# T5 attention and a bilinear feed-forward layer on one core: one weighted-value matmul for both heads' tail queries, and two groups of transposes at other places

## The chip, the core and the metric

The kernel runs on one core of a Trainium2 chip. A core has a matrix engine (TensorE, PE in the profile; its weight loads are listed apart as PEld), three engines for elementwise work (VectorE = DVE, ScalarE = ACT, GpSimd = POOL) and SyncE (SP). Each engine works through its own list of instructions in order and waits on semaphores for the others. Transfers are issued by SP, ACT and POOL and carried by 16 DMA engines. SBUF is the on-chip memory of 128 partitions; PSUM is the memory into which TensorE writes.

The metric is the device time of one execution in microseconds (us). Before the change it is 418.68, the median of four runs.

## What is computed

Attention over 8 batches and 8 heads, 576 positions and head size 64, with a relative-position bias that depends on the distance alone, and then a feed-forward layer without a nonlinearity but the product of its two halves:

```
scores = q @ k.T / sqrt(64) + bias_table[bucket(|i - j|)]   # per batch and head
attn   = exp(scores) / sum(exp(scores))                     # max subtraction cancels
x      = (attn @ v) with heads side by side                 # 4608 x 512
out    = ((x @ w_a) * (x @ w_b)) @ w_out                    # 512 -> 1536 -> 512
```

Beyond a distance of about 128 all positions share the last bucket. The kernel divides the bias of that bucket out, so that only a band around the diagonal has to be multiplied by exp(bias); the whole of it is read from tables `W_sb` and `Wt_sb`.

## The kernel before

**Tiles.** 576 positions are four tiles of 128 (NM = 4) and a tail of 64 (ST). Two heads make a pair, so there are 32 pairs; `p` is a pair, `b, hp = divmod(p, 4)` its batch and its place in it. Scores are computed transposed: keys on the partitions, queries along the columns. For a pair, `qk` (L407) makes for each key tile `t` a PSUM tile `sc` with both heads' 512 main queries, and `ex` (L429, ACT) makes `at` from it with one exponential of 1024 columns; `mul` (L434, DVE) multiplies by the bias table.

**The tail.** The tails of both heads lie together in 128 partitions: head 0 in rows 0 to 63, head 1 in rows 64 to 127. In `ZB` tail queries and tail keys stand block-diagonally. `qk_tail` (L478 to L493) makes the scores of the tail keys, `ex_tail` (L508, L515, L516) their exponentials, into the row buffer `att`. Tail queries against main keys come from `qk` (L416) and `ex_rows` (L423) in later batches, from L485 in the first two. In `att` the columns of these rows are ordered head, key tile, query: 256 columns of head 0 and then 256 of head 1. `mul_tail` (L524) multiplies the band of the tail keys by 192 columns of `Wt_sb`.

**Weighted values.** `av_mm` makes up to three query tiles (`jq`) in one PSUM tile `av`, of which there is one. Each `jq` starts with the tail keys against both heads' tail values (L561, 130 columns: 2 x 65, the 65th being a column of ones that gives the sum), and then adds, per head and key tile, a matmul of 65 columns (L565). That holds for jq = 4, the tail queries, too: there the eight matmuls take from `att` 128 columns at `256 * hh + 64 * t`, of which the first 64 belong to the tile, and only rows 0 to 63 of the result are used. `av_norm` takes the reciprocal of the sums (L579) and multiplies (L580) into `XG[p % 2]`, for jq = 4 by a reciprocal and a product of their own on 64 partitions.

**Transposing x.** `t_x` brings the result, transposed, into `xn_sb`, the operand of the feed-forward layer. For pairs 4 to 30, except 7, SP does it by two DMA transposes (L588, L591). For pairs 0 to 3, 7 and 31 TensorE does it (`tr_x`, L606) through a half of the PSUM tile `trb`, and `copy_x` (L299 on DVE) copies it out. `t_pair` calls it, for pair 7 in two parts one right after the other: tiles 0 to 2, then tiles 3 and 4.

**Transposing q and k.** For batches 0 and 1 TensorE does it. From batch 2 on POOL loads half a batch at a time (`load_half`: k in four pieces, q in four, the tails, v), and `t_half(b, g)` lets SP issue two DMA transposes (L379: `KB` from `kn`, then `QB` from `qn`), for the first half also the tails' (`t_tails`, L371: `ZB` from `tl`). SP's transfers are issued in the order of the program, and a waiting one holds those behind it.

**Order.** The program order is written by hand. The opening, which covers the scores of pairs 0 to 7 and the values of pairs 0 to 5, is a string of tokens: `S`, `T` scores, `E`, `ET` exponentials, `M`, `MT` products, `AV` weighted values, `N` normalisation, `FA`, `FB`, `HA`, `G` feed-forward. Behind `N41` and `N51` come pair 4's and pair 5's `t_x`. After the string `t_half(2, 0)` is called. Then a loop runs over slots `s` = 7 to 32. A slot makes the rest of pair `s`'s scores (`qk(s, ...)`, `qk_tail`) and the weighted values of pair `s - 1`; between them stand places `U` for the feed-forward layer. The layer's work is cut into units: `pa` or `pb` (L630, four matmuls of 512 columns, followed by a copy `ha` on ACT or a product `g` on DVE), and `po` (L667), three units to a tile, the third followed by a copy `ob` (L672) and an output transfer (L675) on ACT. A slot's nine units are dealt evenly over its places:

```
n = (quota * seen + nu - 1) // nu - put
```

**Buffers.** Two PSUM tiles `sc` for scores: a score group can start when the exponential of the last but one has read its tile. One tile `av`: the next weighted-value group waits for the normalisation of the last one.

Of the kernel before, what the change touches and what calls it, by code (L numbers as in the profile page):

```python
# [13 lines left out]
def kernel(  # L14
# [66 lines left out]
    eb_sb = const.tile([128, H], BF16, name="eb_sb")  # L81
    tab_sb = const.tile([128, TB], BF16, name="tab_sb")
    zero_sb = const.tile([128, 512], BF16, name="zero_sb")
    tab = nc.dram_tensor("bias_tab", [H, TB], BF16, kind="Internal")
    NY = S + NM
    W_sb = [wpool.tile([128, 2, NY], BF16, name=f"W{hp}") for hp in range(H // 2)]
    Wt_sb = wpool.tile([128, H // 2, 192], BF16, name="Wt")

# [22 lines left out]
    wb_sb = [wpool.tile([128, NMC, WC], BF16, name=f"wb{i}") for i in range(NW)]  # L111
    wo_sb = wpool.tile([128, NDF, DM], BF16, name="wo")
    xn_sb = [wpool.tile([128, NT], BF16, name=f"xn{mc}") for mc in range(NMC)]
    ob_last = wpool.tile([128, DM], FP32, name="ob_last")
# [87 lines left out]
    def pad_x(i):  # L202
        nc.vector.memset(XG[i][64:128, 4, :, :], 0.0)
        nc.vector.memset(att[i][:, 512 + SM // 2 + ST:], 0.0)

# [39 lines left out]
    def load_wt(hh):  # L245
        nc.gpsimd.dma_start(out=Wt_sb[64 * hh:64 * hh + 64, :, :],
                            in_=bass.AP(tensor=tab, offset=hh * TB + 512,
                                        ap=[[1, 64], [2 * TB, H // 2], [1, 192]]))
# [171 lines left out]
    def ex_rows(p):  # L420
        st[p]["att"] = at = att[p % 2]
        for hh in (1, 0):
            nc.scalar.activation(out=at[:, 256 * hh:256 * hh + 256], in_=st[p]["rows"][hh][:, 0:256],  # L423
                                 func=ACTF.Exp, scale=scale)

# [48 lines left out]
    def qk_tail(p):  # L474
        qT, kT, z = operands(p)
        ps = ps_sc.tile([128, 2, 512], FP32, tag="sc", name=f"qkt{p}")
        if shared(p):
            nc.tensor.matmul(out=ps[:, 0, :], lhsT=z[:, 1, :], rhs=qT[:, :, :], start=True, stop=True)  # L478
            for hh in range(2):
                nc.tensor.matmul(out=ps[:, 1, 0:ST], lhsT=z[:, 1, :], rhs=z[:, 0, ST * hh:ST * hh + ST],  # L480
                                 start=(hh == 0), stop=(hh == 1))
            st[p]["ps"] = (ps, None)
            return
        for t in range(NM):
            nc.tensor.matmul(  # L485
                out=ps[:, 0, :].rearrange("p (h t c) -> p h t c", h=2, t=NM)[:, :, t, :],
                lhsT=kT[:, t, :], rhs=z[:, 0, :], start=True, stop=True)
        n = main_tail(p)
        nc.tensor.matmul(out=ps[:, 1, 0:n], lhsT=z[:, 1, :], rhs=qT[:, (SM - n) // 128:, :],
                         start=True, stop=True)  # L490
        pt = ps[:, 1, n:n + ST] if n < SM else tr_half().bitcast(FP32)[:, 0:ST]
        for hh in range(2):
            nc.tensor.matmul(out=pt, lhsT=z[:, 1, :], rhs=z[:, 0, ST * hh:ST * hh + ST],  # L493
                             start=(hh == 0), stop=(hh == 1))
        st[p]["ps"] = (ps, pt)
# [5 lines left out]
    def ex_tail(p):  # L501
        ps, pt = st[p]["ps"]
        n = main_tail(p)
        at = att[p % 2]
        m = 512 + n
        st[p]["att"] = at
        if shared(p):
            nc.scalar.activation(out=at[:, 512:m + ST],  # L508
                                 in_=ps[:, :, :].rearrange("p a x -> p (a x)")[:, 0:SM + ST],
                                 func=ACTF.Exp, scale=scale)  # L510
            return
        if n < SM:
            m += ST
        else:
            nc.scalar.activation(out=at[:, m:m + ST], in_=pt, func=ACTF.Exp, scale=scale)  # L515
        nc.scalar.activation(out=at[:, 0:m], in_=ps[:, :, :].rearrange("p a x -> p (a x)")[:, 0:m],  # L516
                             func=ACTF.Exp, scale=scale)

    def mul_tail(p):
        if not shared(p):  # L520
            mul_rows(p)
        at, wt = st[p]["att"], Wt_sb[:, p % 4, :]
        o = 512 + main_tail(p) - 128
        nc.vector.tensor_tensor(out=at[:, o:o + 192], in0=at[:, o:o + 192], in1=wt[:, 191::-1], op=MULT)  # L524

    def mul_rows(p):
        at, w = st[p]["att"], W_sb[p % 4]
        x = at[:, 0:512].rearrange("p (h t c) -> p h t c", h=2, t=NM)
        rev = w[:, :, ST - 1::-1]
        e = bass.AP(tensor=rev.tensor, offset=rev.offset,  # L530
                    ap=[rev.ap[0], rev.ap[1], [1, NM], rev.ap[2]])
        nc.vector.tensor_tensor(out=x, in0=x, in1=e, op=MULT)

    def weights(p, t, hh, jq):
        if jq == 4:
            o = 256 * hh + ST * t
            return st[p]["att"][:, o:o + 128]
        if p >= 4:
            return st[p]["at"][t][:, hh, 128 * jq:128 * jq + 128]
        o = 256 * (t % 2) + 128 * (jq % 2)  # L540
        return st[p]["at", jq // 2, t // 2][:, hh, o:o + 128]

    def weights_tail(p, jq):
        if jq == 4:
            o = 512 + main_tail(p)
            return st[p]["att"][:, o:o + 128]
        if p < 4 and jq < 2:
            return atk[:, p, 128 * jq:128 * jq + 128]
        o = 512 + 128 * (jq if p >= 4 else jq - 2)
        return st[p]["att"][:, o:o + 128]  # L550
# [5 lines left out]
    def av_mm(p, jqs, pool=None, tag="av"):  # L556
        b, hp = divmod(p, 4)
        i = b % 2
        pav = (pool or ps_av).tile([128, 3, 2, Dh + 1], FP32, tag=tag, name=f"av{p}_{jqs[0]}")
        for slot, jq in enumerate(jqs):  # L560
            nc.tensor.matmul(out=pav[:, slot, :, :], lhsT=weights_tail(p, jq),  # L561
                             rhs=vt[i][:, hp, :, :], start=True, stop=True)
            for hh in range(2):
                for t in range(NM):
                    nc.tensor.matmul(out=pav[:, slot, hh, :], lhsT=weights(p, t, hh, jq),  # L565
                                     rhs=vm[i][:, 2 * hp + hh, t, :], start=False,
                                     stop=True, skip_group_check=True)
        st[p]["pav", jqs[0]] = pav

    def av_norm(p, jqs):  # L570
        pav = st[p]["pav", jqs[0]]
        rc = wrk.tile([128, 3, 2], FP32, tag="rc", name=f"rc{p}_{jqs[0]}")
        xg = XG[p % 2]
        groups = [(jqs[0], 0, len(jqs), 128)]
        if jqs[-1] == 4:
            groups = [(jqs[0], 0, len(jqs) - 1, 128), (4, len(jqs) - 1, 1, 64)]
        for j0, s0, n, np_ in groups:
            r = rc[0:np_, s0:s0 + n, :]
            nc.vector.reciprocal(out=r, in_=pav[0:np_, s0:s0 + n, :, Dh])  # L579
            nc.vector.tensor_tensor(  # L580
                out=xg[0:np_, j0:j0 + n, :, :], in0=pav[0:np_, s0:s0 + n, :, 0:Dh],
                in1=r.unsqueeze(3).to_broadcast([np_, n, 2, Dh]), op=MULT)

    def t_x(p, jqs=range(5), eng=None):
# [11 lines left out]
        copy_x(p, jqs, eng)  # L596

    def t_pair(p):
        for jqs in ((0, 1, 2), (3, 4)) if p == 7 else (range(5),):
            t_x(p, jqs)  # L600

# [113 lines left out]
    def v_next(s):  # L715
# [15 lines left out]
        N00 TZ0 E301 M100 X00 S201 CX00:D AV10 wa4 E201 M200 N10 CZ0:A M201 X10 TQ11 M301 CX10:A T0 CQ11:A  # L731
        V1:D TQ31 ET0 S111 M010 AV20 E111 MT0 T1 N20 AV30 CQ31:A ET1 M011 TQ21 LH S110 N30 X20 CQ21:A
        S310 CX20:A MT1 X30 E110 AV01 CX30:D M111 FA0a E310 M110 S210 FB0a N01 HA0a S211 E210 FA1a G0a
# [5 lines left out]
        CQ6:A FB2b MT4 E51 TQ7 G2b AV40 CQ7:D E50 TK6 M51 TK7 CK6:A FA3b M50 FB3b HA3b CK7:D S61 G3b T5  # L739
        E61 N40 FA4b FB4b HA4b M61 T6 ET5 G4b AV41 FA5b ET6 N41 S63 FB5b MT5 HA5b S62 E63 FA6b G5b MT6  # L740
        AV50 HA6b M63 E62 S60 FB6b N50 E60 FA7b G6b AV51 M62 HA7b FB7b M60 FA8f G7b N51 FB8f HA8f G8f
# [5 lines left out]
    def step(token):  # L747
# [79 lines left out]
        elif kind == "PC":  # L827
            if p == 2:
                pad_ones(1)
            else:  # L830
                nc.vector.memset(vt[1][64 * p:64 * p + 64, :, 1 - p, :], 0.0)
        elif kind == "PD":
            pad_x(p)
        elif kind == "LH":
            load_half(2, 0)
            load_half(2, 1)
        elif kind == "LV":
            load_vt(2)
        else:
            raise ValueError(token)  # L840
# [3 lines left out]
    pad_tl(1)  # L844
    t_half(2, 0)

    quotas = {7: 9, 8: 9}
    load_slot = {bb: 9 if bb == 3 else 12 if bb == 4 else 4 * bb - 5 for bb in range(3, B)}
    for s in range(7, NP + 1):
# [6 lines left out]
        if new:  # L856
            head = [U, lambda: ex(s, 1), A(0, 1, 2), U, lambda: mul(s, 0), lambda: t_q(s + 1), U,
                    lambda: mul(s, 1)]
            late = [A(3, 4), lambda: t_pair(s - 1), U]
            if shared(s):  # L860
# [67 lines left out]
```

## Time and profile before

| | us |
|---|---|
| median of 4 runs | 418.68 (418.57 to 419.3) |
| the profiled execution's own time | 418.99 |
| its span in the trace | 417.2 |
| DVE, ACT, POOL busy | 237.5, 250.0, 134.1 |

Times below are counted from the span's start. The span is what the program's instructions cover; the profiled execution took 1.8 us more than it. The "busy" share is an average over the whole program; what an engine waits for stands in brackets behind a row of the timeline: idle time before it, and the event that ended it. The granted TensorE clock was 0.998 of the full one.

```profile
L565 PE MATMUL av<-vm,at 128*128 128x65 bf16 x896 | 41.2, 194 | 0.0
L561 PE MATMUL av<-vt,att 128*128 128x130 bf16 x152 | 33.3, 219 | 0.0
L606 PE MATMUL trb<-ident,XG 128*128 128x128 bf16 x30 | 3.6, 219 | 2.0 <-DVE xn L299 1.1 <-ACT xn L297 0.4 <-DVE XG L580 0.3
L480 PE MATMUL qkt<-ZB 128*128 128x64 bf16 x48 | 5.3, 193 | 0.0
```

These are rows of the table of groups by line and shape: line, engine, operation, output and inputs, shapes and count, then the group's busy time in us and the mean length of one in ns, then idle time before it and what ended it. The length of a matmul runs from its start to its modelled end, with its way through the array, so neighbours overlap; what a matmul takes from the engine is the distance between starts.

### The profile page before, as it was taken

Reading aid. Unit: us, or ns where it says so; the run is one execution under the profiler, and the core shown is the slowest. Engines: PE = TensorE matmul, PEld = TensorE weight load, DVE = VectorE, ACT = ScalarE, POOL = GpSimd, SP = SyncE. Lnnn points to the kernel's source line nnn. Section 1 sums busy time; section 2 is a strip of 40 time slices with the busy share of each in tenths; the row PEclk is TensorE's granted clock in tenths of the full one; section 3 lists DMA queues with packets and bytes.
Section 4 is the critical chain, followed back from the end, with each engine's and each line's share of the span. In section 5 each row is a group of like instructions: output and inputs, shape, how many; then the busy total and the mean of one; then the engine's idle time right before and its main releaser. Section 6 shows DMA issues by size and latency. Waiting matters only on the chain.

```text
span 417.2 us, 9172 instructions
## 1 busy us (share of the span) xinstructions
PE 404.9 (97%) x3657; PEld 211.9 (51%) x3657; DVE 237.5 (57%) x569; ACT 250.0 (60%) x388; POOL 134.1 (32%) x191
## 2 busy tenths in 40 slices
PE   8789999799999999999999999999999999999996
PEld 3467665445554554455555555545545554444443
DVE  6778886447654766467636674566546662430420
ACT  4988876386656675576657764866566742322321
POOL 7957455299209600790049102500000000000000
PEclk9999999999999999999999999999999999999999
DMA  8999999999949981998099906950420012002004
GB/s 112 170 209 197 205 136 157 154 137 144 127 91 151 125 94 38 159 143 116 18 140 159 130 16 133 130 91 17 91 90 16 17 41 75 2 0 101 2 0 101
DMA packets 135787, 42.07 MB, mean 101 GB/s; under 512 B 113688, under 2 KB 130968, under 8 KB 135744
## 3 DMA queue, kind: packets, MB, share of 16 engines
q0 software_dynamic: 81712, 20.27, 54.2%
q1 hardware_dynamic: 48592, 11.87, 19.3%
q10 hardware_dynamic: 5440, 9.34, 6.9%
q8 instruction: 28, 0.46, 0.5%
q14 instruction: 15, 0.12, 0.1%
HBM read 39.18 MB, written 9.45 MB: 117 GB/s over the span
## 4 chain that ended last, share of the span: by engine, by line
PE 87%; DMA 6%; POOL 3%; issue 1%; ACT 1%; DVE 1%; ACTq 0%; SPq 0%
PE pb L630 22%; PE pa L630 21%; PE po L667 21%; PE av L565 8%; PE qk L407 7%; DMA wb<-in_moe_w_b_dram 2%; DMA QB<-qn 2%; PE av L561 2%; PE qkt L478 1%; DMA kn<-in_k_dram 1%; POOL W L236 1%; DMA bias_tab<-tab_sb 1%; PE trb L307 1%; PE trb L416 1%; PE warm L221 1%
## 5 line engine op out<-in xcount | busy, mean ns | idle before, releaser
L429 ACT ACTIVATE at<-qk 128x1024 bf16<-128x1024 f32 x112 | 113.4, 1029 | 30.6 <-PE qk L407 13.1
L640 DVE TENSOR_TENSOR g<-pb,ha 128x512 bf16<-128x512 f32 (+1 forms) x116 | 75.9, 655 | 75.8 <-PE pb L630 47.5
L630 PE MATMUL pb<-xn,wb 128*128 128x512 bf16 (+1 forms) x464 | 112.5, 365 | 0.8 <-DMA wb<-in_moe_w_b_dram 0.8
L630 PE MATMUL pa<-xn,wa 128*128 128x512 bf16 (+1 forms) x464 | 112.5, 365 | 0.0
L637 ACT ACTIVATE ha<-pa 128x512 f32<-128x512 f32 (+1 forms) x116 | 66.6, 574 | 65.9 <-PE pa L630 65.8
L667 PE MATMUL po<-wo,g 128*128 128x512 bf16 x420 | 98.7, 379 | 0.0
L434 DVE TENSOR_TENSOR at<-at,W 128x1024 bf16<-128x1024 bf16 x112 | 74.8, 684 | 20.8 <-ACT at L429 20.8
L630 PEld LDWEIGHTS <-wa 128*128 128x128 bf16 x464 | 41.7, 98 | 45.7 <-issue 6.5
L630 PEld LDWEIGHTS <-wb 128*128 128x128 bf16 x464 | 40.9, 98 | 42.2 <-issue 4.7
L667 PEld LDWEIGHTS <-g 128*128 128x128 bf16 x420 | 38.3, 98 | 43.0 <-issue 2.5
L579 DVE RECIPROCAL rc<-av 128x6 f32<-128x6 f32 (+3 forms) x96 | 16.3, 170 | 51.9 <-PE av L565 51.6
L672 ACT ACTIVATE ob<-po 128x512 f32<-128x512 f32 x35 | 21.0, 600 | 39.3 <-PE po L667 32.6
L170 POOL DMA_DIRECT2D vt<-in_v_dram x12 | 8.1, 691 | 108.6 <-PE av L565 108.6
L565 PE MATMUL av<-vm,at 128*128 128x65 bf16 x896 | 41.2, 194 | 0.0
L565 PEld LDWEIGHTS <-at 128*128 128x128 bf16 x896 | 37.2, 98 | 6.2
L132 POOL DMA_DIRECT2D qn<-in_q_dram x48 | 36.6, 834 | 8.9 <-PE qk L407 8.4
L580 DVE TENSOR_TENSOR XG<-av,rc 128x384 bf16<-128x384 f32 (+3 forms) x96 | 36.2, 377 | 3.3
L141 POOL DMA_DIRECT2D kn<-in_k_dram x48 | 36.4, 810 | 1.8 <-PE trb L362 1.4
L561 PE MATMUL av<-vt,att 128*128 128x130 bf16 x152 | 33.3, 219 | 0.0
L407 PE MATMUL qk<-QB,KB 64*128 64x512 bf16 x192 | 29.1, 381 | 1.1 <-DMA QB<-qn 1.1
L508 ACT ACTIVATE att<-qkt 128x576 bf16<-128x576 f32 x24 | 15.6, 648 | 13.1 <-PE qkt L480 13.1
L561 PEld LDWEIGHTS <-att 128*128 128x128 bf16 x152 | 15.0, 98 | 6.3
(103 smaller groups left out, 315.0 us busy)
## 6 DMA issues: line engine op xcount, KB each, us to landing
out_dram<-ob ACTq DMA_DIRECT2D x32, 256.0 KB, 2.8
vn<-in_v_dram POOLq DMA_DIRECT2D x16, 256.0 KB, 5.4
kn<-in_k_dram POOLq DMA_DIRECT2D x48, 64.0 KB, 4.6
qn<-in_q_dram POOLq DMA_DIRECT2D x48, 64.0 KB, 3.8
wa<-in_moe_w_a_dram POOLq DMA_DIRECT2D x3, 512.0 KB, 9.2
wb<-in_moe_w_b_dram POOLq DMA_DIRECT2D x3, 512.0 KB, 9.5
wo<-in_moe_w_out_dram POOLq DMA_DIRECT2D x1, 1536.0 KB, 15.5
xn<-XG SPq DMA_TRANSPOSE x52, 2.9
```

The lines of the kernel that those rows point to most:

```text
L132: nc.gpsimd.dma_start(out=by_tile(qn[b % 2])[:, h0 // 4, t, :, :], in_=q[b, h0:h1, 128 * t:128 * t + 128, :].transpose([1, 0, 2]))
L141: nc.gpsimd.dma_start(out=by_tile(kn[b % 2])[:, h0 // 4, t, :, :], in_=k[b, h0:h1, t:SM:NM, :].transpose([1, 0, 2]))
L407: nc.tensor.matmul(out=ps[:, hh, :], lhsT=kT[r, t, :], rhs=qT[r, :, :], start=True, stop=True)
L429: nc.scalar.activation(out=at[:, :, :], in_=ps[:, :, :], func=ACTF.Exp, scale=scale)
L434: nc.vector.tensor_tensor(out=at[:, :, :], in0=at[:, :, :], in1=w[:, :, S - 1 + t:S - 1 + t - SM:-1], op=MULT)
L561: nc.tensor.matmul(out=pav[:, slot, :, :], lhsT=weights_tail(p, jq), rhs=vt[i][:, hp, :, :], start=True, stop=True)
L565: nc.tensor.matmul(out=pav[:, slot, hh, :], lhsT=weights(p, t, hh, jq), rhs=vm[i][:, 2 * hp + hh, t, :], start=False, stop=True, skip_grou ...
L580: nc.vector.tensor_tensor(out=xg[0:np_, j0:j0 + n, :, :], in0=pav[0:np_, s0:s0 + n, :, 0:Dh], in1=r.unsqueeze(3).to_broadcast([np_, n, 2, ...
L630: nc.tensor.matmul(out=ps[:, 0:n], lhsT=w[df // 4][:, mc, 128 * (df % 4):128 * (df % 4) + 128], rhs=xn_sb[mc][:, 512 * c + lo:512 * c + lo ...
L637: nc.scalar.activation(out=ha[:, 0:n], in_=ff["pa", df, lo][:, 0:n], func=ACTF.Copy)
L640: nc.vector.tensor_tensor(out=g_sb[df][:, lo:lo + n], in0=ff["pb", df, lo][:, 0:n], in1=ff["ha", df, lo][:, 0:n], op=MULT)
L667: nc.tensor.matmul(out=po[:, :], lhsT=g_sb[df][:, 128 * tt:128 * tt + 128], rhs=wo_sb[:, df, :], start=(df == 0), stop=(df == NDF - 1))
```

## The change

- **Weighted values of the tail queries.** The rows of `att` are reordered from head, tile, query to tile, head, query. For jq = 4 one matmul per key tile takes 128 columns of `att` (both heads' 64 tail queries) against both heads' values (130 columns), in place of one per head and key tile: five matmuls where there were nine. The products of one head's queries with the other head's values are computed too and not used. The result of head 0 stands in rows 0 to 63, that of head 1 in rows 64 to 127, so the normalisation takes one reciprocal for all tiles and a product per head for the last one. The tail keys' part of `att` gets 128 query columns in place of 64: one score matmul of 128 columns instead of two of 64, exponentials 64 columns longer, `mul_tail` 256 columns instead of 192. `Wt_sb` grows to 256 columns; the first 64 are copied from the next 64 (token `PW`).
- **Batch 2's transposes** `t_half(2, 0)` are called by a token `TH` behind `N41` in the opening, and no longer after it. On SP's queue they move past pair 5's two transfers.
- **Pair 7's transposes**: in slot 8 a place for a unit stands between the weighted values of tiles 3 and 4 and the transposes of tiles 0 to 2, and one between these and those of tiles 3 and 4. Slot 8 has ten places instead of nine, and still nine units.
- The bias table's staging tile `tab_sb` becomes a part of `wo_sb`, which is loaded later, and a memset of `att` goes.

```diff
-    Wt_sb = wpool.tile([128, H // 2, 192], BF16, name="Wt")
+    Wt_sb = wpool.tile([128, H // 2, 256], BF16, name="Wt")
...
+    tab_sb = wo_sb[:, :, :].rearrange("p a b -> p (a b)")[:, 0:TB]
...
-            for hh in range(2):
-                nc.tensor.matmul(out=ps[:, 1, 0:ST], lhsT=z[:, 1, :], rhs=z[:, 0, ST * hh:ST * hh + ST],
-                                 start=(hh == 0), stop=(hh == 1))
+            nc.tensor.matmul(out=ps[:, 1, 0:2 * ST], lhsT=z[:, 1, :], rhs=z[:, 0, :],
+                             start=True, stop=True)
...
-            nc.scalar.activation(out=at[:, 512:m + ST],
-                                 in_=ps[:, :, :].rearrange("p a x -> p (a x)")[:, 0:SM + ST],
+            nc.scalar.activation(out=at[:, 512:m + 2 * ST],
+                                 in_=ps[:, :, :].rearrange("p a x -> p (a x)")[:, 0:SM + 2 * ST],
...
-        nc.vector.tensor_tensor(out=at[:, o:o + 192], in0=at[:, o:o + 192], in1=wt[:, 191::-1], op=MULT)
+        nc.vector.tensor_tensor(out=at[:, o:o + 256], in0=at[:, o:o + 256], in1=wt[:, 255::-1], op=MULT)
...
+    def weights_last(p, t):
+        return st[p]["att"][:, 2 * ST * t:2 * ST * t + 2 * ST]
...
+            if jq == 4:
+                for t in range(NM):
+                    nc.tensor.matmul(out=pav[:, slot, :, :], lhsT=weights_last(p, t),
+                                     rhs=vm[i][:, 2 * hp:2 * hp + 2, t, :], start=False,
+                                     stop=True, skip_group_check=True)
+                continue
...
+        for hh in range(2 if m < n else 0):
+            rows = slice(ST * hh, ST * hh + ST)
             nc.vector.tensor_tensor(
...
+                out=xg[0:ST, 4, hh, :], in0=pav[rows, m, hh, 0:Dh],
+                in1=rc[rows, m, hh:hh + 1].to_broadcast([ST, Dh]), op=MULT)
...
-        E61 N40 FA4b FB4b HA4b M61 T6 ET5 G4b AV41 FA5b ET6 N41 S63 FB5b MT5 HA5b S62 E63 FA6b G5b MT6
+        E61 N40 FA4b FB4b HA4b M61 T6 ET5 G4b AV41 FA5b ET6 N41 TH S63 FB5b MT5 HA5b S62 E63 FA6b G5b MT6
...
+        elif kind == "PW":
+            nc.vector.tensor_copy(out=Wt_sb[:, :, 0:64], in_=Wt_sb[:, :, 64:128])
...
+        elif kind == "TH":
+            t_half(2, 0)
...
     pad_tl(1)
-    t_half(2, 0)
...
-            late = [A(3, 4), lambda: t_pair(s - 1), U]
+            late = [A(3, 4), lambda: t_x(s - 1), U]
+            if s == 8:
+                late = [A(3, 4), U, lambda: t_x(7, (0, 1, 2)), U, lambda: t_x(7, (3, 4))]
```

## The prediction

> **What bounds the kernel now.** I read the busy table, then the slices, then the chain that ended last.
>
> ```profile
> PE 404.9 (97%) x3657; PEld 211.9 (51%) x3657; DVE 237.5 (57%) x569; ACT 250.0 (60%) x388; POOL 134.1 (32%) x191
> ...
> PE   8789999799999999999999999999999999999996
> ...
> PE 87%; DMA 6%; POOL 3%; issue 1%; ACT 1%; DVE 1%; ACTq 0%; SPq 0%
> ```
>
> TensorE is the bound; the slices show where it is not full: the first 30 us and the eighth slice (73 to 83 us). So I took the timeline of TensorE and compared each matmul's start with the next one's: 512 columns take 216 ns from start to start, 130 columns 55 to 56, 65 columns 29 to 35. From 83 us to the end no matmul starts more than 0.10 us later than this pitch. Between 60 and 83 us two do, and the timeline names both:
>
> ```profile
> 75.16 0.61 PE L407 MATMUL qk<-QB,KB 64*128 64x512 bf16 x4 [1.08 <-DMA QB<-qn]
> ...
> 81.28 0.27 PE L606 MATMUL trb<-ident,XG 128*128 128x128 bf16 x2 [1.07 <-DVE xn L299]
> ```
>
> The bracket is idle time counted from the modelled end. By starts: the last `po` matmul before the first row starts at 73.70, so the row was due at 73.70 + 0.216 + 0.10 (the usual pause ahead of 64-row matmuls) = 74.01; it lost **1.15 us**. Before the second row, the third transpose started at 79.99 and the fourth at 81.28, where 0.055 is the pitch: **1.23 us**.
>
> **Part 1, shared weighted-value matmuls.** The last-tile slot (jq 4) of each pair is one 130-column and eight 65-column matmuls:
>
> ```profile
> 204.81 0.22 PE L561 MATMUL av<-vt,att 128*128 128x130 bf16 x1
> 204.86 0.42 PE L565 MATMUL av<-vm,att 128*128 128x65 bf16 x8
> 205.12 1.02 PE L630 MATMUL pb<-xn,wb 128*128 128x512 bf16 x4
> ```
>
> From the first start to the next group: 205.12 − 204.81 = 0.314 us with the third decimals. The columns stay 650, so only the cost per instruction goes: eight starts cost 8 x 32.5 = 260 ns, although 65/512 of the 216 ns pitch is 27.4. The weight loads (L565 PEld) stand at the same 32 to 33 ns, so I read the excess as the weight load's own pitch. Four matmuls of 130 columns: 4 x 56 = 224 if they behave as L561 and the transposes L606 (55 ns each, a load each) do. Gain 36 to 37 ns a pair. Bounds, since two 65-column pieces with a gap in one operand are not in the trace: no gain if each costs two old ones (65 ns); 38 ns at best. I take 37.
>
> *A rule against it.* The Trainium skill (TensorE: Matmul & The Clock Gate, "Back-to-back issue gap") says that in a stream of weight-load and matmul pairs 128 columns go at about 81 ns each, not at columns over clock. Four would then be 324 ns: a loss of 64 ns a pair. The rows here, loads included, give 55 to 56 in runs of three and four (L606, L485), so the trace decides; by the rule the part would be +1.7 us instead of −1.0.
>
> Pairs 5 to 31 have this slot on the filled TensorE: 27 x 37 ns = **1.00**. Pairs 0 to 4 lie in the opening; what is saved before the 10.4 us wait for `wb` (the chain has it at 17.77 to 28.19) is lost, and after it five small waits on ACT and DVE (35 to 57 us, 0.1 to 0.3 us each by starts) eat some: **0.05**, with −0.15 to +0.15 as ends, since the exponentials there get 64 columns longer. The tail's two 64-column score matmuls (28 + 29 ns) become one of 128 (55.5): 27 x 1.5 ns = **0.04**.
>
> What the edit adds elsewhere. ACT: L508 goes from 576 to 640 columns, +54 ns (0.648 for 576, 1.024 for 1024, so 0.84 ns a column); the two row exponentials write in four pieces of 64, which I cost at nothing. DVE: L524 192 to 256 columns, some +50 ns; the normalisation stays four instructions (one reciprocal instead of two, two 64-row products instead of one). Cover: the next score matmul writes the PSUM tile that L508 read. Over all loop slots the smallest distance between that end and that start is 0.23 us, in slots 8, 12, 16..., about 0.05 of it the hand-over. So 54 ns fits; beyond 0.18 the excess would be paid in five further slots. DVE has 43% idle. The copy "PW" (a 128x256 copy on DVE, near 22 us, ahead of pair 0's tail product) waits for a load for which the next instruction waits anyway; cover is TensorE's 0.97 us wait at 27.2. The table's new place in `wo` adds a wait on a transfer that ended near 7 us to a load issued at 40.6: nothing, as are two small memsets that leave DVE's start.
>
> **Part 2, batch 2's transposes earlier.** Before, they stand on SP's queue behind pair 5's two transfers:
>
> ```profile
> 62.21 1.22 SPq L588 DMA_TRANSPOSE xn<-XG  x1
> 63.54 1.16 SPq L591 DMA_TRANSPOSE xn<-XG  x1
> 64.94 1.25 SPq L379 DMA_TRANSPOSE KB<-kn  x1
> 66.37 1.81 SPq L379 DMA_TRANSPOSE QB<-qn  x1
> 68.42 2.02 SPq L371 DMA_TRANSPOSE ZB<-tl  x1
> ```
>
> QB landed 8.7 us after 66.37, at 75.02: the late operand. Moved, the three follow pair 4's transfers, which are issued by 58.48. What holds them then is their data. The last `kn` piece (issued 45.27, 12.6 to landing) is there at 57.9. The last `qn` piece is late, on POOL's queue behind `wo` (40.62, 15.5 to landing, 56.1):
>
> ```profile
> 56.67 0.74 POOL L132 DMA_DIRECT2D qn<-in_q_dram  x1 [6.87 <-PE qk L407]
> ```
>
> It lands 4.4 later, at 61.0. So KB 58.5, QB 61.1, ZB 63.3 (the last `tl` is issued at 59.22 and lands 4.0 later). With the same 8.7 us, QB lands at 69.8: 4.2 ahead of 74.01. The whole **1.15** goes; next late would be the PSUM tile of the second score group, free when L516 ends at 73.53 against 74.23. ACT then has its `ob` copy and its DMA issue (to 75.09) ahead of the first exponential, 0.65 late; nothing waits for it before the third group, which has 6.6 us in this slot.
>
> Behind ZB stand pair 5's transfers: 65.4 and 66.7 in place of 62.2 and 63.5, landing at 71 to 75. Their readers: chunk 1's matmuls at 88, and pair 7's normalisation, which overwrites XG at about 76.5. Pair 6's are due at 70.7 as before.
>
> **Part 3, pair 7's transposes a unit apart.** The 1.23 us is one row of dependent DVE work after the last weighted-value matmul (reciprocal, product, reciprocal, product, copy: 80.08 to 81.22) before the second transposes. Two units of 0.865 us now cover it: the second transposes come 0.865 + 0.17 + 0.865 = 1.9 us after that matmul, and the work takes 1.4. But nine units are now dealt over ten places, so the last place of slot 8 gets none, and the tail matmuls have one unit behind them where they had two. There the next slot's second score group waits for L508. ACT in this slot before:
>
> ```profile
> 83.64 1.02 ACT L429 ACTIVATE at<-qk 128x1024 bf16<-128x1024 f32 x1 [3.59 <-PE qk L407]
> 84.56 0.38 ACT L423 ACTIVATE att<-qr 128x256 bf16<-128x256 f32 x1
> 84.82 0.39 ACT L423 ACTIVATE att<-trb 128x256 bf16<-128x256 f32 x1
> 85.09 0.62 ACT L672 ACTIVATE ob<-po 128x512 f32<-128x512 f32 x1
> 85.73 0.34 ACTq L675 DMA_DIRECT2D out_dram<-ob  x1
> 86.12 1.02 ACT L429 ACTIVATE at<-qk 128x1024 bf16<-128x1024 f32 x1 [0.41 <-ACT ob L672]
> 87.04 0.65 ACT L508 ACTIVATE att<-qkt 128x576 bf16<-128x576 f32 x1
> ```
>
> The `ob` copy moves ahead of the third exponential, as its unit does. With the slot's first matmul at 74.01: that unit ends at 81.57, `ob` starts 0.20 later, and ACT is free 1.03 after that, 82.80. Exponential, rows, exponential take 3.40 − 1.03 = 2.37 to the start of L508, 85.17; it ends 0.70 later, 85.87, and hands over at 85.92. The score group was due 4.70 after the third one (83.21 to 87.91); one unit less makes 3.83, from 81.67: 85.50. New stall **0.4** (0 to 0.7). Net **0.83**.
>
> **Sum.** 1.00 + 0.05 + 0.04 + 1.15 + 0.83 = 3.07. The profiled execution took 418.99 (span 417.2 and 1.8 around it): 415.9. It lies 0.3 above the median 418.68, so for the median **415.6**.
>
> **Rivals.**
> 1. *Only part comes through*: merged matmuls at 65 ns (−1.0), or the new stall eats part 3 (−0.8), or the opening's exponentials lengthen its waits. 416.0 to 416.8. For it: the two-piece operand and ACT's order are not in the trace. Chance 0.18.
> 2. *The moved transposes don't pay*: DMA engines are 99% busy there; should QB take over 12.9 us, the wait stays. Against it: it took 8.7 at its worst here. 418.68 − 1.92 = 416.8. Chance 0.09.
> 3. *The 81 ns rule holds*: 418.68 − (1.15 + 0.83 + 0.04 − 1.7) = 418.4. Chance 0.06.
> 4. *Slower: pair 5 behind ZB on SP.* Its transfers hold XG; pair 7's normalisation waits, holds the only weighted-value PSUM tile, and TensorE stops ahead of the next group, due at 78.1. The normalisation needs 0.8, so it decides from a landing after 77.3; each us later costs one, and after 80.4 the gain is gone. At 82, 420.3. For it: saturated DMA, and ZB is the longest issue (2.02). Against it: 15 us of flight would be needed, and the longest transpose near is 9.3. Chance 0.06.
>
> The forecast has 0.61, own range 415.0 to 416.2. 0.2% is 0.84 us, about what a measurement tells from no change. Faster by more: 0.61 + 0.18 + 0.09 = 0.88, less 0.02 for partial cases that add up: 0.86. Same: rival 3 and those, 0.08. Slower: 0.06. The range to 417.2 takes in rivals 1 and 2; below, all gains in full without the stall give 418.68 − 3.6 = 415.1, and 0.4 for the measurement, 414.7.
>
> **What would show it.** Part 1: slot of jq 4 at 0.28 us, L565's successor at 56 ns from start to start; 65 or 81 refutes it. Part 2: QB issued near 61, landed before 74, no idle time before the first `qk<-QB,KB`. Part 3: no wait on `xn` before the second transposes, and a new idle time of about 0.4 us near 85.5, before the third `qk<-QB,KB` group, released by L508's successor. Wrong altogether if a wait of over 1 us stands on XG near 76 or if the batch period, 44.09 us, does not fall by about 0.15.

## The result

The changed kernel takes 416.72 us, the median of 40 runs (415.72 to 418.23), against 419.22 for the kernel before on the same chips, the median of 59 runs (417.48 to 422.79). The ratio is 0.9942, with a 95% interval of 0.9932 to 0.9952: 2.0 to 2.9 us less. The forecast was 415.6 and 3.07 less. The time lies above the forecast's own range (415.0 to 416.2) and inside the wider one that takes in the rivals (to 417.2).

### The profile page after: what moved, and what is told of

Its sections match the earlier page's. It is cut to its first block, busy times and chain, and to the rows that moved or that the text cites. A ratio compares the mean times of both kernels' runs of the same rounds, so it can differ in the third digit from the quotient of the medians.

```text
span 415.9 us, 8826 instructions
## 1 busy us (share of the span) xinstructions
PE 404.9 (97%) x3497; PEld 211.1 (51%) x3497; DVE 240.8 (58%) x568; ACT 251.4 (60%) x388; POOL 133.5 (32%) x191
## 4 chain that ended last, share of the span: by engine, by line
PE 91%; ACT 5%; DMA 1%; issue 1%; DVE 1%; ACTq 0%; POOL 0%; POOLq 0%
PE pa L633 23%; PE pb L633 23%; PE po L670 21%; PE av L569 8%; PE qk L406 7%; PE av L559 2%; ACT ath L452 2%; PE av L563 2%; PE qkt L479 1%; DMA qn<-in_q_dram 1%; PE trb L306 1%; ACT att L514 1%; PE warm L220 1%; PE trb L415 1%; PE trb L609 1%
## 5 line engine op out<-in xcount | busy, mean ns | idle before, releaser
L643 DVE TENSOR_TENSOR g<-pb,ha 128x512 bf16<-128x512 f32 (+1 forms) x116 | 75.9, 654 | 74.2 <-PE pb L633 46.1
L580 DVE RECIPROCAL rc<-av 128x6 f32<-128x6 f32 (+1 forms) x64 | 11.9, 186 | 49.4 <-PE av L569 43.8
L406 PE MATMUL qk<-QB,KB 64*128 64x512 bf16 x192 | 29.2, 381 | 0.2 <-ACT att L506 0.2
L582 DVE TENSOR_TENSOR XG<-av,rc 128x384 bf16<-128x384 f32 (+1 forms) x64 | 27.1, 424 | 2.2
L506 ACT ACTIVATE att<-qkt 128x640 bf16<-128x640 f32 x24 | 16.9, 702 | 12.9 <-PE qkt L480 12.9
L452 ACT ACTIVATE ath<-qkh 128x1024 bf16<-128x1024 f32 x16 | 15.7, 1045 | 4.8 <-PE qkh L446 4.8
```

What stands on the lines that cost most here:

```text
L406: nc.tensor.matmul(out=ps[:, hh, :], lhsT=kT[r, t, :], rhs=qT[r, :, :], start=True, stop=True)
L582: nc.vector.tensor_tensor(out=xg[:, jqs[0]:jqs[0] + m, :, :], in0=pav[:, 0:m, :, 0:Dh], in1=rc[:, 0:m, :].unsqueeze(3).to_broadcast([128, ...
L643: nc.vector.tensor_tensor(out=g_sb[df][:, lo:lo + n], in0=ff["pb", df, lo][:, 0:n], in1=ff["ha", df, lo][:, 0:n], op=MULT)
```

## The profile after

The profiled execution took 417.75 us (span 415.9). From its page, the engines' busy time, TensorE's slices and the chain that ended last:

```profile
PE 404.9 (97%) x3497; PEld 211.1 (51%) x3497; DVE 240.8 (58%) x568; ACT 251.4 (60%) x388; POOL 133.5 (32%) x191
...
PE   7799999999999999999999999999999999999996
...
PE 91%; ACT 5%; DMA 1%; issue 1%; DVE 1%; ACTq 0%; POOL 0%; POOLq 0%
```

There are 160 matmuls fewer: 128 weighted-value ones and 32 tail scores. The eighth slice is full now, and DMA's share of the chain has gone from 6% to 1%. That TensorE's busy time is the same is no contradiction: each matmul counts to its modelled end, which overlaps the next start, and for 3.4 us of the opening the matmuls ran at half the clock (see below). The first slice holds more waiting than before, 7 tenths busy instead of 8. The timeline of TensorE shows the places that the forecast named. First, the scores that waited for QB and the last-tile slot in the filled part:

```profile
75.43 0.61 PE L406 MATMUL qk<-QB,KB 64*128 64x512 bf16 x4
...
203.97 0.22 PE L559 MATMUL av<-vt,att 128*128 128x130 bf16 x1
204.02 0.40 PE L563 MATMUL av<-vm,att 128*128 128x130 bf16 x4
204.26 0.59 PE L633 MATMUL pb<-xn,wb 128*128 128x512 bf16 x2
```

No bracket stands behind the first row: the wait for QB is gone. The slot takes 204.26 − 203.97, with the third decimals 0.290 us, where it took 0.314; 0.28 was forecast. Second, pair 7's two groups of transposes and the next slot's first two score groups:

```profile
80.98 0.33 PE L609 MATMUL trb<-ident,XG 128*128 128x128 bf16 x3
...
82.01 0.28 PE L609 MATMUL trb<-ident,XG 128*128 128x128 bf16 x2
...
86.74 0.39 PE L406 MATMUL qk<-QB,KB 64*128 64x512 bf16 x2
87.34 0.39 PE L406 MATMUL qk<-QB,KB 64*128 64x512 bf16 x2 [0.20 <-ACT att L506]
```

The transposes wait for nothing. The second score group starts 0.60 behind the first, where 0.22 is usual: **0.38 us** of new wait, released by the tail's exponential (now L506), as the forecast had it (0.4). ACT in that slot:

```profile
83.18 0.60 ACT L675 ACTIVATE ob<-po 128x512 f32<-128x512 f32 x1 [2.88 <-PE po L670]
83.81 0.34 ACTq L678 DMA_DIRECT2D out_dram<-ob  x1
84.20 1.02 ACT L430 ACTIVATE at<-qk 128x1024 bf16<-128x1024 f32 x1 [0.42 <-PE qr L415]
...
86.55 0.73 ACT L506 ACTIVATE att<-qkt 128x640 bf16<-128x640 f32 x1
```

The `ob` copy stands ahead of the third exponential and pushes it. The tail's exponential ends 4.20 us after the third score group's start (83.08); the forecast had 85.87 − 81.67 = 4.20.

SP's queue, from the same trace:

```profile
59.99 1.25 SPq L378 DMA_TRANSPOSE KB<-kn  x1
62.30 1.23 SPq L378 DMA_TRANSPOSE QB<-qn  x1
64.51 2.02 SPq L370 DMA_TRANSPOSE ZB<-tl  x1
66.63 2.28 SPq L595 DMA_TRANSPOSE xn<-XG  x1
69.01 1.18 SPq L598 DMA_TRANSPOSE xn<-XG  x1
```

Everything in this profile is about 1.4 us later at this point than in the one of before (on that below). QB landed at 69.85, 5.6 us ahead of its reader at 75.43. Pair 5's transfers, now behind ZB, landed at 74.5 and 75.9; the normalisation that overwrites XG, due near 78, did not wait.

**Where the time went.** I paired each of ACT's copies of a feed-forward result with the same copy of the kernel before and followed the difference of their ends along the trace:

| place | after minus before, us | step |
|---|---|---|
| 46 us | +1.37 | opening |
| 75 us (last `po` ahead of QB's reader) | +1.42 | |
| 78 us (behind QB's reader, by TensorE's starts) | +0.27 | −1.15: part 2 |
| 90 us | −0.62 | −0.84 by starts, pair 7's own slot in it: part 3 |
| 121 us | −0.66 | |
| 414 us | −1.21 | −0.64 from pair 8 on (by starts): part 1, 24 pairs |

Parts 2 and 3 have the forecast sizes. Part 1 is 26.6 ns a pair, not 37 + 1.5. The period of a batch, four pairs, says the same: by the starts of the tail scores it is 43.99 us where it was 44.09, 0.107 less; the forecast had 0.15. And 1.4 us are lost ahead of 27 us, where the change does next to nothing: in this execution the first `qn` load landed at 6.9 us, in the one of before at 5.5. The runs below say more of that.

## The experiments

There are twelve runs of eleven kernels. All but the two measuring kernels and the first reordered one compute the whole output.

**Parts 2 and 3 undone, one at a time.**

```diff
-... AV41 FA5b ET6 N41 TH S63 FB5b ...
+... AV41 FA5b ET6 N41 S63 FB5b ...
...
     pad_tl(1)
+    t_half(2, 0)
```

> The changed kernel with one part undone: batch 2's transposes stand after the opening again, behind pair 5's transfers on SP. Theory (the wait for QB is worth 1.15 us by itself): the matmul behind the last po ahead of the first qk<-QB,KB starts about 1.15 to 1.25 us late again, everything behind it is that much later against the changed kernel, and pair 7's part keeps its 0.84 us. Rival (the wait was hidden by something else that is late as well): under 0.5 us comes back. It also repeats the opening's first 30 us: if the 1.4 us that the changed kernel's profile lost there is chance in when the first q load lands, this run need not show it; if the change causes it, it is there.

One run: 420.75 us. TensorE's timeline:

```profile
76.86 0.61 PE L406 MATMUL qk<-QB,KB 64*128 64x512 bf16 x4 [2.51 <-DMA QB<-qn]
```

The wait is back, but twice as long as in the kernel before: SP issued QB at 67.1 and it landed 9.6 later, at 76.7. And it cost more than itself. Busy time by stretches of the same trace (stretch, length, then busy us and instructions of TensorE, its weight loads, DVE, ACT and POOL, the granted clock, the DMA share, GB/s; a transfer counts in full where it starts, so the share can exceed 1):

```profile
74.00:78.00 4.00, 1.49 (x9) 0.45 (x8) 0.51 (x2) 1.31 (x2) 0.00 (x0) 0.99 1.59 150
78.00:81.30 3.30, 3.08 (x32) 2.24 (x31) 0.80 (x3) 1.23 (x2) 0.00 (x0) 0.50 1.03 247
```

From 1.1 us behind the wait TensorE had half its clock, 0.50, for 3.4 us: the 65-column matmuls start some 55 ns apart there and those of 512 columns 430. In the profile of before the wait was 1.1 us and the clock stayed at 1.00. The Trainium skill (TensorE: Matmul & The Clock Gate, "HAM oscillation") has such a gate close on gaps beyond some 3.4 us; here it closed behind 2.5 us of idle time. That the wait closed it is likely from the order of the two, but its length alone does not decide: in two openings the half clock came behind 1.3 and 1.0 us, in others gaps of up to 1.9 us passed without it (the list at the end). The half clock costs about 1.6 us more, which I did not foresee. The opening was 0.3 us behind the profile of before, not 1.4. So part 2 is not always worth the same; the same kernel timed:

> The changed kernel with batch 2's transposes behind the opening again, timed. Its single look lost 3 us, not 1.2: QB landed 9.6 us after an issue at 67.1 and TensorE waited 2.6 us for it. Theory (the wait's length differs from run to run with the DMA engines' load, and the part's worth is its mean, 1.2 to 3 us): ratio to the kernel before 0.997 to 1.002, a spread of its times as wide as that of the kernel before. Rival (the single look was an outlier and the part is worth 1.15): 0.996 to 0.998.

418.18 us, median of 10 (417.01 to 418.73), beside 418.89 for the kernel before (417.25 to 422.71): ratio 0.9976, interval 0.9950 to 1.0003. In this run's profile QB landed at 74.53 and the reader was 0.47 late (0.57 less the usual 0.10). So the wait is between 0.5 and 2.6 us in three profiled executions of one order (1.15 in the kernel before), and nothing where the transposes are moved. The difference to the changed kernel's ratio is 0.0034 or 1.4 us, near the 1.15 that I took; the two intervals just overlap (0.9950 against 0.9952), so that mean is not sharp. The first execution was an extreme one: its 420.75 lies above all ten timed ones. The spread is not as wide as that of the kernel before, so that part of the expectation failed, and nothing here ties the wait to the longest times of the kernel before (its three longest of 59 are 421.6 to 422.8, the changed kernel's longest of 40 is 418.2). Nor is the half clock behind the longest one beside this run: 422.71 had a mean granted clock of 1.000, where the execution with the long wait had 0.996. What makes those times is open.

```diff
-                late = [A(3, 4), U, lambda: t_x(7, (0, 1, 2)), U, lambda: t_x(7, (3, 4))]
+                late = [A(3, 4), lambda: (t_x(7, (0, 1, 2)), t_x(7, (3, 4))), U]
```

> The changed kernel with pair 7's two groups of transposes side by side again; slot 8 then has nine places for nine units. Theory: the 1.23 us wait between the third and fourth transpose is back, and the 0.4 us wait in the next slot's second score group is gone, so TensorE is 0.8 us later behind slot 8. Rival (the 0.4 us wait comes from the 64 longer columns of the tail's exponential and not from the missing unit): the 0.4 us stays and the loss is 1.2. The opening's loss of 1.4 us: not there if chance.

One run: 417.21 us. From TensorE's timeline, the second transposes and the next slot's scores:

```profile
80.15 0.27 PE L609 MATMUL trb<-ident,XG 128*128 128x128 bf16 x2 [1.18 <-DVE xn L298]
...
86.56 0.61 PE L406 MATMUL qk<-QB,KB 64*128 64x512 bf16 x4
```

The wait for the chain of DVE work is back (1.34 us by starts) and the four score matmuls stand together again, though the tail's exponential still has its 64 longer columns. So the missing unit makes the 0.38, not the columns. TensorE is 0.97 us later behind slot 8 than in the changed kernel, counted from the copy at 75 us; the forecast had 0.83, and the wait is 0.1 longer here than in the kernel before.

**The 0.38 us taken back.** If nine units meet nine places, it should go:

```diff
             if s == 8:
+                head = head[1:]
                 late = [A(3, 4), U, lambda: t_x(7, (0, 1, 2)), U, lambda: t_x(7, (3, 4))]
```

> The changed kernel with slot 8's first place for a unit left out, so that nine units meet nine places and the last place has one again. Theory: the 0.38 us wait of the second score group of slot 9 goes, pair 7's transposes still wait for nothing, TensorE is 0.3 to 0.4 us earlier behind slot 8. Rival (the early place covered something else, the products that pair 7's weighted values need): a wait of some tenths appears before the weighted values of pair 7, and nothing is gained.

One run: 415.52 us. On TensorE:

```profile
79.32 0.28 PE L609 MATMUL trb<-ident,XG 128*128 128x128 bf16 x2
...
84.88 0.61 PE L406 MATMUL qk<-QB,KB 64*128 64x512 bf16 x4
```

Four score matmuls together, no bracket, and no wait ahead of pair 7's weighted values. From the copy at 75 us to the one at 90 this kernel gains 2.41 us on the kernel before, the changed one 2.04: 0.37 recovered.

**Why a merged matmul takes 58.9 ns.** A matmul's time here is the distance from its start to the next one's. The forecast had 56, on the reading that the 65-column starts are held to 32.5 by their weight loads. The changed kernel's trace gives 60.4, 58.5, 58.3 and 58.2 for the four, while the 130-column matmul that opens a slot takes 56. I took other causes: the place of the operand, and adding to PSUM columns that the matmul just before wrote.

```diff
-    vm = [wpool.tile([128, H, NM, Dh + 1], BF16, name=f"vm{i}") for i in range(2)]
+    vm = [wpool.tile([128, H, NM, Dh + 2], BF16, name=f"vm{i}") for i in range(2)]
...
-                                     rhs=vm[i][:, 2 * hp:2 * hp + 2, t, :], start=False,
+                                     rhs=vm[i][:, 2 * hp:2 * hp + 2, t, 0:Dh + 1], start=False,
```

> The values' tile has 66 columns a head and key tile instead of 65, so that every 65-column piece starts at a multiple of 4 bytes; nothing else differs from the changed kernel. Theory A (the 2.9 ns by which a 65-column matmul starts later than its columns say, and the 2.5 ns of the merged ones, come from operand pieces at odd places): runs of 65 go from 32.5 to about 29.6 ns from start to start, merged ones from 58.5 to 56, some 3 us in all. Theory P (it comes from adding to the PSUM columns that the matmul just before wrote): no change. Theory W of the prediction (the pitch of weight loads): no change.

```diff
+        for t in range(NM):
             for hh in range(2):
-                for t in range(NM):
-                    nc.tensor.matmul(out=pav[:, slot, hh, :], lhsT=weights(p, t, hh, jq),
+                for slot, jq in enumerate(jqs):
+                    if jq < 4:
+                        nc.tensor.matmul(out=pav[:, slot, hh, :], lhsT=weights(p, t, hh, jq),
...
+                    elif hh == 0:
+                        nc.tensor.matmul(out=pav[:, slot, :, :], lhsT=weights_last(p, t),
```

> The same weighted-value matmuls in another order: key tile outermost, then head, then query tile, so that no matmul adds to the PSUM columns that the one just before it wrote. Theory P: 65-column starts go from 32.5 to about 29.6 ns and the merged ones from 58.5 to 56, some 3 us in all. Theory A (odd places of the operand) and theory W (pitch of weight loads): pitch unchanged, time the same.

This first reordered kernel does not keep all of the sums: each tile's first matmul carries a start flag, which comes before the other tiles have added up. The number and kind of its matmuls is the same. The next one sets the flag for the first tile alone, which keeps them, and adds the 66 columns:

```diff
-                             rhs=vt[i][:, hp, :, :], start=True, stop=True)
+                             rhs=vt[i][:, hp, :, :], start=(slot == 0), stop=True,
+                             skip_group_check=slot > 0)
```

> Both at once: pieces of the values at multiples of 4 bytes and the order in which no matmul adds to the columns that the one just before it wrote; only the first query tile's first matmul of a group carries the start flag, so that the others keep their sums. The two single runs gave 32.0 and 30.2 ns for a 65-column start (32.4 before). Theory (the two causes are separate, the order the larger): 29.2 to 29.8 ns, merged ones at 57 to 58, group of three tiles 0.89 us, of two 0.58; span 0.3 to 0.8 us below that of the reordered run at the same opening. Rival (only the order counts): 30.2 ns and no more.

```diff
-    vm = [wpool.tile([128, H, NM, Dh + 1], BF16, name=f"vm{i}") for i in range(2)]
+    vm = [wpool.tile([128, H // 2, NM, 2, Dh + 1], BF16, name=f"vm{i}") for i in range(2)]
...
-                                     rhs=vm[i][:, 2 * hp:2 * hp + 2, t, :], start=False,
+                                     rhs=vm[i][:, hp, t, :, :], start=False,
```

> The values' tile laid out with both heads of a pair side by side for each key tile, so that the merged matmul reads 130 columns in one piece at a multiple of 4 bytes; order and all else as in the changed kernel (the copy into it is done in two instructions instead of one). Theory (the 2.6 ns above 56 that a merged matmul takes come from its operand being two pieces): merged starts at 56 ns, slot of the last tile 0.280 us. Rival (they come from adding to columns just written): 58 to 59 ns as before, 57.6 if only the places of the pieces count.

Mean distance between starts from 90 to 345 us, in ns, and the median length of a group of three query tiles and of the last two:

| kernel | 65 columns | merged, 130 | three tiles | two tiles | one run's time, us |
|---|---|---|---|---|---|
| before | 32.4 | – | 948 | 631 | 418.99 |
| changed | 32.4 | 58.9 | 948 | 608 | 417.75 |
| align66 | 31.9 | 57.6 | 935 | 599 | 416.49 |
| inter | 30.2 | 61.4 | 904 | 593 | 415.77 |
| inter66 | 30.0 | 59.8 | 898 | 586 | 414.48 |
| pairlay | 30.3 | 59.0 | 900 | 592 | 415.52 |

Most 65-column starts in the last three are at 29.2, a few at 31 to 35. That takes the weight load out of the list for 65 columns: there are as many loads as before, one for each matmul. The reordered kernels seemed to speak for PSUM, but `pairlay` keeps the sequential order, adds to just-written columns every time, and is as fast. Theory P falls, and theory A as I put it (multiples of 4 bytes) explains 0.5 of 2.9 ns. What `pairlay` and the reordered kernels share is the place of the values from one matmul to the next: 260 bytes on, or the same place again, instead of 130 or 132 bytes on. The merged matmuls did not follow: one piece instead of two (`pairlay`) leaves 59.0, so its theory, the two pieces alone, fails. Two measuring kernels were to separate the causes.

```diff
+        kind = p % 4
...
+                tv, tw = (0 if kind == 0 else t), (0 if kind == 2 else t)
...
+                nc.tensor.matmul(out=pav[:, slot, hh, :], lhsT=weights(p, tw, hh, jq),
+                                 rhs=vm[i][:, 2 * hp + hh, tv, :], start=(kind == 1),
```

> A measuring kernel, sequential order as in the changed kernel. Every fourth pair is left as it is; of the others, one kind reads the values of key tile 0 in all its weighted-value matmuls, one sets the start flag in all of them so that they overwrite instead of adding, and one uses the weights of key tile 0 for all: these parts of the sums are left out or replaced. Only starts are read, 32.4 ns for 65 columns and 58.9 merged in the untouched kind. If the place of the values in SBUF sets the surcharge, the first kind falls to 29.2 and about 56; if adding in PSUM does, the second; if the place of the weights does, the third. What no kind moves stays open.

| kind of pair | 65 columns, last two tiles, ns | merged, ns | three tiles, us |
|---|---|---|---|
| values of one place | 30.3 | 59.1 | 0.87 |
| start flag in all | 32.5 | 58.8 | 0.92 |
| weights of one place | 32.4 | 58.8 | 0.91 |
| untouched | 32.6 | 58.9 | 0.92 |

Here the three tiles are counted from the first start to the last one. The place of the values decides for 65 columns; adding in PSUM does not, nor does the place of the weights. The merged ones, still in two pieces, stay where they are in all four.

```diff
+                    tv = (0, t % 2, t, t)[kind]
...
+                                     rhs=vt[i][:, hp, :, :] if kind == 3 else vm[i][:, hp, tv, :, :],
```

> A second measuring kernel, sequential order, both heads' values side by side so that a merged matmul reads one piece. By pair: all weighted-value matmuls read the values of key tile 0; or of tiles 0 and 1 in turn; or as they should; or the tail's values, as the first matmul of each slot does: in three of four pairs these values are replaced in the sums. Only starts are read. Theory (a change of place from one matmul to the next costs, and two pieces are one such change): merged starts at 56 to 57 ns in the first and last kind, 59 in the untouched one; 65 columns at 29 ns in the first and last. Rival (the surcharge of the merged ones has nothing to do with the operand's place): 58 to 59 in all four.

Here both heads' values lie side by side, so a merged matmul reads one piece of 260 bytes a partition. Six pairs of each kind lie between 90 and 345 us; of the last two tiles:

| kind of pair | 65 columns, ns | the four merged in order, ns | their mean |
|---|---|---|---|
| values of one place | 30.4 | 56.7, 56.7, 56.3, 56.7 | 56.6 |
| two places in turn | 30.2 | 56.5, 61.0, 55.5, 59.5 | 58.1 |
| as they should be | 30.5 | 56.7, 60.8, 59.2, 59.2 | 59.0 |
| the tail's values | 31.0 | 56.0, 56.7, 56.7, 56.7 | 56.5 |

One slot of the first kind (pair 8) and one of the third (pair 10), each up to the next group:

```profile
93.31 0.22 PE L561 MATMUL av<-vt,att 128*128 128x130 bf16 x1
93.37 0.39 PE L566 MATMUL av<-vm,att 128*128 128x130 bf16 x4
93.60 0.59 PE L637 MATMUL pb<-xn,wb 128*128 128x512 bf16 x2
...
115.18 0.22 PE L561 MATMUL av<-vt,att 128*128 128x130 bf16 x1
115.24 0.40 PE L566 MATMUL av<-vm,att 128*128 128x130 bf16 x4
115.48 0.81 PE L637 MATMUL pb<-xn,wb 128*128 128x512 bf16 x3
```

With the third decimals the two slots take 0.283 and 0.293 us; the forecast had 0.28. So for the merged matmuls the theory holds and the rival falls: **the surcharge of the merged matmuls comes from their operand.** It goes when the values are one piece and stand at the place that the matmul before read. For the 65 columns the kinds hardly differ, so the 29 ns of that theory did not come. One piece at new places leaves the merged ones at 59.0 (third kind, `pairlay`), and one place in two pieces leaves 59.1 (`mixed`, first kind), so both count. The second kind shows where it falls: on the second and fourth matmul, which step 260 bytes on, and not on the third, which steps back. Why a step on, or a second piece, costs 2 to 4 ns is **open**.

**A faster version.** The reordering with 66 columns and slot 8's place, and the same with the values side by side:

> A version meant to be faster than both: the changed kernel with values at multiples of 4 bytes, the reordered weighted-value matmuls and slot 8's first place left out. From the single traces: reordering and places 1.7 us behind slot 8 and 0.3 ahead of it, the slot 0.38. Against the changed kernel 2.2 to 2.6 us less; ratio to the kernel before 0.987 to 0.990. If the gains do not add, 0.991.

> The same with the values laid out with both heads of a pair side by side instead of 66 columns a piece: in sequential order that layout alone brought the 65-column starts from 32.4 to 30.3. With the reordering 29.2 to 30 ns; ratio to the kernel before 0.987 to 0.990, within 0.001 of the other version.

414.56 and 414.73 us, medians of 6 runs each, against 420.01 for the kernel before in the same rounds: ratios 0.9867 (0.9842 to 0.9892) and 0.9873 (0.9852 to 0.9894). The changed kernel's interval, 0.9932 to 0.9952, lies above both. Reordering adds nothing for the 65 columns to the side-by-side layout (30.8 ns, three tiles 906, as against 900 in order), so that layout or the order is enough, not both. In `bestpair`, which computes the whole output, a merged matmul reads one piece that begins where the matmul before it began to read, and the last three of the four take 55.9, 56.0 and 55.8 ns, as the measuring kernel has it (58.5 to 59.2 in two pieces, `best66`); the first takes 61.7, which nothing here explains.

**The opening.** At the copy at 46 us the kernels with the changed opening stand between −0.5 and +1.5 us of the one profile of before: no_p3 −0.1, no_th 0.2, align66 0.6, the faster version 1.5, unit8 −0.5, the changed one 1.4. With one and the same opening the first `qn` load landed at 5.4 in one and at 6.9 in another. In the changed kernel's profile the late load left TensorE idle for 1.7 us, and the clock fell behind it, from the same view by stretches of that trace:

```profile
8.00:12.00 4.00, 3.61 (x36) 1.19 (x35) 1.75 (x6) 1.62 (x2) 3.41 (x6) 0.61 0.76 108
```

In no_p3, with the load at 5.7, it is 1.00 there. Up to 46 us the changed kernel's opening is the same as that of no_th, no_p3 and unit8, which lost 0.2, −0.1 and −0.5, so its 1.4 is chance in the main. That the late load and the half clock make it up is not shown: unit8 had the clock at 0.51 from 11.8 to 15.3 us and was the earliest of all, inter with its load at 6.8 and a full clock lost 0.95, and the faster version with its load at 6.1 and a full clock 1.5. Whether some tenths belong to the change can't be told: there is one profile of the kernel before.

## Right or wrong, by the forecast's own steps

1. *TensorE is the bound from 83 us on, so what it saves is saved.* Right: the differences along the trace keep what a stage gains to the end, and there is no new wait but one.
2. *Part 1: 4 x 56 ns, gain 37 ns and 1.5 for the tail scores.* The mechanism is right, **the size is wrong**: 58.9 ns instead of 56. The slot went from 314.7 to 291.4 ns, so 23.3 instead of 37; the tail scores brought 1.6 as forecast. Over 27 pairs that is 0.7 us instead of 1.04. The failed step is the reading that the excess over 65/512 of the 216 ns pitch was the weight load's own pitch and would hide behind 130 columns. The runs show that for 65 columns the values' place makes it, and that a merged matmul has an excess of its own, from its two pieces and from their step from one matmul to the next: without both it takes the 56 to 57 ns that were forecast. The forecast named the two pieces as not in the trace, and its rival 1 priced them at 65 ns; the step it did not think of. The 81 ns of the skill's rule were much further off on the other side: these runs, a load for every matmul, give 56 to 64.
3. *Part 2: 1.15.* Right in this pair of profiles (1.15), and the reasons as well: QB's issue waited for the last `qn` piece and not for pair 5. What I did not see is that the wait differs between executions, 0.5 to 2.6 us in the three profiled (QB's flight at its old place took 7.8 to 9.6 us), and that the clock can fall to half behind a long one. I took one execution's wait for the wait; that the timed mean (1.4, not sharp) came near it is in part luck. The "99% busy" of the second rival says more than the profile: the digit 9 of its DMA row is 90% or more.
4. *Part 3: 1.23 less a new 0.4.* Right: 1.23 gone, 0.38 new, at the place, by the engine and for the reason given; moving the place for the unit took it back.
5. *What the edit adds elsewhere is covered.* Right: but for the 0.38 in slot 9 no group of scores in slots 9 to 31 starts late, although ACT's tail exponential went to 0.70 us and DVE's busy time rose by 3.3.
6. *Opening 0.05.* Not to be told; chance moves it by more than a microsecond.
7. *Pair 5 behind ZB (slower).* It landed at 75.9 against 77.3, from where it would have cost: in that execution all was 1.4 later, so the margin was nearer 2.8. It did not bite in any run.

Parts 1 to 3 as measured give 0.7 + 1.15 + 0.81 = 2.7 us; the medians differ by 2.5, within the interval of 2.0 to 2.9. Of the rivals, the first came nearest: the forecast of 415.6 was 1.1 too low, mostly since 0.3 were missing in part 1 and the medians of this series lie 0.5 above the four runs that it started from.

## What to carry to other kernels

On a filled engine the gain of fewer and longer instructions is read from start to start, and an excess in that pitch needs a cause that has been tried: here laying the two heads' values side by side was worth more than the merge (between 90 us and the end, `pairlay` gains 2.0 us on the kernel before, the changed kernel 0.6). When units are dealt over places, a place added in one stage takes a unit from another, and what stood behind it must be looked up by name. A wait for a transfer under full DMA load is one draw out of a range (0.5 to 2.6 us here), and on TensorE a long draw can cost more than its length: the one of 2.6 us had half the clock behind it, at some 1.6 us more.

## What the runs showed of the hardware

- Consecutive 65-column matmuls, each with its weight load, start 32.4 ns apart when their moving operands lie 130 bytes apart in a partition (31.9 at 132 bytes), and mostly 29.2 when they lie 260 bytes apart or at one place. At 130 bytes it is 32.5 too when they overwrite in PSUM instead of adding. Why the distance counts is open.
- 130-column matmuls, each with its weight load, run at 56 to 57 ns when they open a slot, at 56.7 three in a row in the reordered kernels, and at 56.5 to 56.6 four in a row when each reads one piece of 260 bytes at the place of the one before. Four in a row take 59.0 when the piece moves on by 260 bytes, and 57.6 to 59.1 when it is two pieces, moved or not. Why is open as well.
- Half the clock, for 3.4 us each time, followed idle times of TensorE of 2.5 us (no_th), 1.7 us (the changed kernel's opening), and 1.3 and 1.0 us (the openings of unit8 and mixpair). It did not follow the 1.1 us of the kernel before, nor 1.34 us in the openings of ten kernels, nor 1.9 us at 27 us in `bestpair`. The length of the idle time alone does not decide.
- The same DMA transpose (QB) took 7.1 to 9.6 us to land in the window from 60 to 77 us, where the digit of the DMA row is 9.
